# First batch's attention on four sets of buffers: q and k of all four jobs loaded ahead of v, the mask added by TensorE

## The chip, the cores and the metric

One Trainium2 chip, of which the kernel uses one core. The metric is the time of one execution on the device in microseconds (us). Three executions of the kernel before gave 918.25, 918.97 and 919.79 us; the median is 918.97 us.

## The reference

Inputs: q, k, v of shape (4 batches, 8 heads, 576 positions, 64), and the weights of two feed-forward layers, all float32.

```
q_d, k_d, v_d = means over 4 neighbouring positions          # 144 of them
out_d  = softmax(q_d k_d^T / 8) v_d ; out_up = each row of out_d repeated 4 times
mask   = |pos_i - pos_j| < 4
scores = where(mask, q k^T / 8, -1e9) ; out_local = softmax(scores) v
x = (out_up + out_local) laid out as (2304 tokens, 512)
x = (sigmoid(x Wg) * (x Wv)) Wo                              # layer 1, 1536 hidden
h = x Win ; out = (h * sigmoid(1.702 h)) Wout                # layer 2, 2048 hidden
```

So each batch first goes through a pooled (full) and a banded (local) attention, and the 2304 tokens then go through two gated layers. The large products are made as three float32r matmuls each (high times high, high times low, low times high).

## The kernel before, in words

**Two kinds of work.** The attention of batch b is four jobs, one for each pair of heads (`Job(b, hp)`, hp 0 to 3). A job loads q and k, pools them by four (`pool4`), makes the banded scores with 96 small matmuls (`scores`, L674), adds the mask and takes the softmax, makes the pooled scores with 8 matmuls (`down` or `pooled`, L724) and their softmax (`pooled_softmax`), transposes the pooled weights (`down_t`, L784), and multiplies both with v (`band`, L799, and `values`, L821). The sum of both (L834) is split into a high and a low part, `xhi` and `xlo` (L845, L847): slice hp of the input of layer 1. v of the first batch is pooled by 24 matmuls for each half of the heads (`Values.pool_tiles`, L592) with a matrix `ones`.

The layers are "visits". The first visit takes batch 0 through layer 1: for each of 12 pieces f of the hidden width, 24 matmuls of 512 columns make gate and value (`hidden`, L939 to L941, into `ph`), and 12 more the piece of the output (`result`, into `acc`). Each weight arrives as 64-bit words, is converted by ACT and DVE (`convert`, L865, L867, L869), and split into `whi` (ACT, L876) and `wlo` (DVE, L879). The attention of batches 1 to 3 is mixed into the visits before theirs.

**Where things lie.** Buffers are handed out in turn from named rings: `qt` and `kt` have two places each, `sc` one, `pt`, `tt`, `pd`, `xf`, `qd` and `kd` two, `pdt` and `half` one. Jobs 2 and 3 of batch 0 load q and k into the last four weight tiles (`qt0`, `kt0`), whose weights come later. All other buffers of batch 0 are those that later batches use.

**What sets the order.** `Plan` collects every operation with an engine, a cost, a due time and the buffers it reads and writes, and `Plan.order` lays them out one engine at a time by due times and its own costs; the program then holds that order on each engine. `T0` is the time for which the planner plans the first visit; `Job.t0`, `Job.due` and the constants at L514 ff. give the due times. Where the planner sees PE idle in the beginning it puts in fillers, bf16 matmuls on a tile `warm` whose result nobody reads (L1433). All loads and stores go through SP's queue, in the planner's order.

For a job of batch 0 the softmax of the band is: DVE adds the mask to the scores in PSUM and writes `sc` (L693), takes the maxima (L707), subtracts (L708); ACT takes the exponential into `pt` (L711); DVE sums (L712), inverts (L714), scales (L715) and transposes (L716) into `tt`.

```
            masked = self.b == 1
            def scored():
                for h in range(2 if masked else 0):
                    nc.tensor.matmul(ss.t[:, h, :n], identb.t, maskb, start=True, stop=False, skip_group_check=True)
```

In batch 1 (`masked`) the mask is instead put into PSUM by a matmul with the identity ahead of the scores (L668), and DVE reads maxima and differences from PSUM.

Of the kernel before, what the change touches and what calls it, by code (L numbers as in the profile page):

```python
# [288 lines left out]
def tile_multiscale_attention_gated_ffn(  # L289
# [9 lines left out]
    nc = tc.nc  # L299
# [86 lines left out]
    first = [x.rearrange("p a b -> p (a b)").bitcast(F32) for x in top[-4:]]  # L386
    firsts = [Slot(x[:, :n]) for x, n in zip(first, (S + 8, KPAD + S + 5) * 2)]
    plan.ring("qt0", firsts[::2])
    plan.ring("kt0", firsts[1::2])
    for n, x in enumerate(wslots[-8:]):  # L390
        x.under = (firsts[n // 2],)
# [8 lines left out]
    qslots, kslots, vslots, pslots = (plan.rings[nm][0] for nm in ("qt", "kt", "vt", "pt"))  # L400
# [70 lines left out]
    for s in [*qslots, *plan.rings["qt0"][0]]:  # L471
        nc.vector.memset(s.t[:, S:], 0.0)
    for s in [*kslots, *plan.rings["kt0"][0]]:
        nc.vector.memset(s.t[:, :KPAD], 0.0)
        nc.vector.memset(s.t[:, KPAD + S:], 0.0)
# [40 lines left out]
    T0 = 37.0e3  # L516
# [3 lines left out]
    EARLY = 16.0e3  # L520
    AHEAD = 15.0e3
    FIRST = ((-14.0e3, 14.0e3), (-13.0e3, 16.0e3), (-12.0e3, 18.0e3))
# [19 lines left out]
    class Values:  # L542
# [6 lines left out]
        def load(self):  # L549
            b, c = self.b, slice(self.c0, self.c0 + VC)  # L550
            if b:
                self.vt, self.vd, self.vg = buf("vt"), buf("vd"), buf("vg")

            hp = self.job.hp
            d, after = (self.job.t0 - 3000.0, self.job.t0 - 12000.0) if b else (4500.0 * hp, 4500.0 * hp)
            for kh in range(2) if b else ():
                dma(self.vg.t[:, kh], v[b, kh * 4 * GH:(kh + 1) * 4 * GH, c].rearrange("(g r) d -> g r d", r=4),
                    GH * 4 * VC * 4, [], [(self.vg, kh)], d, after)
            d, after = (self.job.due(0.2), self.job.t0 - 9000.0) if b else (4000.0 * hp, 4000.0 * hp)
            if not b:  # L560

                if hp:
                    return
                c, n, t, d, after = slice(0, DM), 2, vboth.rearrange("p g h c -> p g (h c)"), -19.2e3, 3.5e3
# [12 lines left out]
            row = NQ * (NT - 1) - 3  # L577
            dma(t[96:96 + S - row, NG - 1], v[b, row:S, c], (S - row) * n * VC * 4, [], [(x, 5) for x in bs],
                d, after)

        def pool_tiles(self):
# [3 lines left out]
            at = self.job.due(0.55)  # L585
# [22 lines left out]
    class Job:  # L608


        def __init__(self, b, hp):
            self.b, self.hp = b, hp
            if b == 0:
                a, z = -EARLY, T0 - EARLY
            else:
                a, z = visits[b - 1]["t"] - LEAD, visits[b]["t"] - (SLACK if b < B - 1 else SLACK7)
            step = (z - a) / NHP
            self.t0, self.t1 = a + hp * step, a + (hp + 1.6) * step
            self.banks = twos if b == 0 else twos[:1]
            self.merged = b > 0 and (b, hp) != (1, 0)  # L620
# [3 lines left out]

        def load(self):
            b, hp = self.b, self.hp
            early = b == 0 and hp > 1
            self.qt, self.kt = (buf("qt0"), buf("kt0")) if early else (buf("qt"), buf("kt"))
# [29 lines left out]
        def scores(self):  # L658
# [5 lines left out]
            masked = self.b == 1  # L664
# [15 lines left out]
            if not self.merged:  # L680
                op("pe", 1500.0 + 200.0 * masked, scored, [qt, kt, *[identb][:masked]], [ss, sc], when)
# [56 lines left out]
        def pooled_softmax(self, ss, c, at, masked):  # L738

            nmd, smd, pd = self.nmd, self.smd, self.pd  # L740
            op("dve", dve_ns(4 * G), lambda: nc.vector.reduce_max(
                nmd.t.rearrange("p (h r) -> p h r", h=2),
                ss.t[:GH, :, c:c + 2 * G].rearrange("p h (r k) -> p h r k", k=G), axis=AX.X),
               [ss, *masked], [nmd], at)
            op("act", 200.0, lambda: nc.scalar.mul(nmd.t, nmd.t, -SCALE_D), [], [nmd], at)
# [23 lines left out]
        def down_t(self):  # L769
            self.pdt = buf("pdt")  # L770
# [32 lines left out]
        def values(self):  # L803
# [21 lines left out]
            xf = buf("xf")  # L825
# [28 lines left out]

    def convert(src, out, due, at=None, after=None):

        w = buf("w64")
        if at is None:
# [3 lines left out]
        def words(n, dtype=I32):  # L862
# [3 lines left out]
            out.t.bitcast(F32), words(1, F32), AF.Prelu, scale=2.0 ** -112, alpha=-2.0 ** 32), [w], [out], due)  # L866
        op("act", act_ns(DM), lambda: nc.scalar.activation(  # L867
# [510 lines left out]
    def make_ones():  # L1378
        nc.gpsimd.memset(ones.t, 0.0)
        for i in range(4):  # L1380
            c = 30 + 36 * (i % 2)
            part = ones.t[32 * i:32 * i + 32, c:c + 6]
            nc.gpsimd.memset(part, 1.0)
            nc.gpsimd.affine_select(out=part, in_=part, pattern=[[-4, 6]], compare_op=ALU.is_ge,
                                    fill=0.0, base=-3, channel_multiplier=1)
            nc.gpsimd.affine_select(out=part, in_=part, pattern=[[4, 6]], compare_op=ALU.is_ge,
                                    fill=0.0, base=6, channel_multiplier=-1)

    op("pool", 1500.0, make_ones, [], [ones], -4.0e3)
# [89 lines left out]
```

## Time and profile before

| what | us |
|---|---|
| median of three executions (918.25 to 919.79) | 918.97 |
| the profiled execution, its own time | 919.47 |
| its span, first to last instruction | 917.8 |
| PE busy | 907.8 (99%) |
| DVE busy | 691.3 (75%) |
| ACT busy | 544.0 (59%) |
| POOL busy | 80.5 (9%) |
| chain that ended last: share of PE | 98% |

The busy time of an engine is the time in which an instruction of its own runs, whether anybody needs the result or not: PE's 907.8 us hold the fillers too. The profiled execution took 919.47 us, of which 917.8 us are its span and 1.67 us lie around it.

### The profile page before, as it was taken

The numbers are of one execution on the slowest core, as the hardware profiler recorded it, in microseconds if no ns is written. First come the engines' busy times: TensorE is split into PE (matmuls) and PEld (weight loads), VectorE is DVE, ScalarE is ACT, GpSimd is POOL, SyncE is SP. The second block draws the span as 40 slices with busy tenths as digits, with TensorE's granted clock in tenths as the row PEclk, the third lists the DMA queues.
The fourth block names the chain that finished last, engine by engine and source line by source line (L and its number), as shares of the span: only waits on it lengthen the run. The fifth ranks groups of instructions, "written<-read, shape, count | busy, mean of one in ns | idle before, by whom it ended". The sixth has DMA issues, their size and how long they took to land.

```text
span 917.8 us, 18930 instructions
## 1 busy us (share of the span) xinstructions
PE 907.8 (99%) x7392; PEld 761.9 (83%) x7392; DVE 691.3 (75%) x1291; ACT 544.0 (59%) x1163; POOL 80.5 (9%) x124
## 2 busy tenths in 40 slices
PE   8999999999999999999999999999999999999998
PEld 4678888888888887889999998888888988888886
DVE  4777776776576766799999898878976779877742
ACT  4788885656666666665545655545665655535541
POOL 6221100111011100010000000000301001000000
PEclk9999999999999999999999999999999999999999
DMA  9559672574365734434311751002531002000431
GB/s 286 139 193 261 197 216 57 164 213 148 126 190 181 237 116 145 153 109 141 108 51 41 223 196 46 37 33 73 193 125 70 1 1 69 35 35 35 167 98 47
DMA packets 63949, 113.76 MB, mean 124 GB/s; under 512 B 8241, under 2 KB 29563, under 8 KB 63858
## 3 DMA queue, kind: packets, MB, share of 16 engines
q1 hardware_dynamic: 63858, 112.54, 38.7%
q8 instruction: 58, 0.95, 0.4%
q14 instruction: 33, 0.27, 0.1%
HBM read 82.37 MB, written 30.15 MB: 123 GB/s over the span
## 4 chain that ended last, share of the span: by engine, by line
PE 98%; POOL 1%; issue 0%; DVE 0%; POOLq 0%
PE ph L939 14%; PE ph L940 13%; PE ph L941 13%; PE acc L939 9%; PE acc L941 8%; PE acc L940 8%; PE pa L940 7%; PE pa L939 7%; PE pa L941 7%; PE pa L799 2%; PE pa L674 1%; PE pa L724 1%; PE acc L1433 1%; PE pa L821 1%; PE pa L784 1%; PE acc L799 1%
## 5 line engine op out<-in xcount | busy, mean ns | idle before, releaser
L939 PE MATMUL ph<-xhi,whi 128*128 128x512 f32 (+1 forms) x344 | 135.1, 393 | 0.0
L940 PE MATMUL ph<-xhi,wlo 128*128 128x512 f32 (+1 forms) x344 | 131.6, 383 | 0.0
L941 PE MATMUL ph<-xlo,whi 128*128 128x512 f32 (+1 forms) x344 | 131.5, 382 | 0.0
L876 ACT CAST whi<-w 128x512 fp32r<-128x512 f32 x140 | 85.5, 612 | 59.9 <-PE ph L941 33.2
L879 DVE TENSOR_TENSOR wlo<-w,whi 128x512 fp32r<-128x512 f32 x137 | 95.4, 698 | 29.7 <-ACT whi L876 29.3
L879 DVE TENSOR_TENSOR wlo<-wr,whi 128x512 fp32r<-128x512 f32 x106 | 69.8, 660 | 41.2 <-ACT whi L876 39.9
L939 PEld LDWEIGHTS ph<-xhi,whi 128*128 128x128 f32 x344 | 64.7, 188 | 15.2 <-issue 2.1
L941 PEld LDWEIGHTS ph<-xlo,whi 128*128 128x128 f32 x344 | 64.8, 188 | 12.9
L876 ACT CAST whi<-wr 128x512 fp32r<-128x512 f32 x106 | 60.2, 570 | 25.2 <-PE acc L941 12.2
L940 PEld LDWEIGHTS ph<-xhi,wlo 128*128 128x128 f32 x344 | 64.9, 189 | 11.7
L939 PE MATMUL acc<-ghi,whi 128*128 128x512 f32 (+1 forms) x192 | 73.7, 384 | 0.0
L941 PE MATMUL acc<-glo,whi 128*128 128x512 f32 (+1 forms) x192 | 72.3, 377 | 0.5 <-DVE glo L879 0.5
L1053 DVE TENSOR_TENSOR w<-pa,w 128x512 f32<-128x512 f32 (+1 forms) x112 | 70.4, 629 | 2.4 <-PE pa L941 1.9
L940 PE MATMUL acc<-ghi,wlo 128*128 128x512 f32 (+1 forms) x192 | 72.2, 376 | 0.0
L876 ACT CAST w<-w 128x512 fp32r<-128x512 f32 x62 | 37.9, 619 | 43.1 <-PE acc L940 23.6
L940 PE MATMUL pa<-w,wlo 128*128 128x512 f32 (+1 forms) x166 | 60.6, 365 | 0.0
L941 PE MATMUL pa<-w,whi 128*128 128x512 f32 (+1 forms) x166 | 60.6, 365 | 0.0
L939 PE MATMUL pa<-w,whi 128*128 128x512 f32 (+1 forms) x166 | 60.6, 365 | 0.0
L879 DVE TENSOR_TENSOR w<-w,w 128x512 fp32r<-128x512 f32 x58 | 41.2, 716 | 19.0 <-ACT w L876 18.9
L973 ACT ACTIVATE th<-ph 128x512 f32<-128x512 f32 (+1 forms) x44 | 24.6, 559 | 39.2 <-PE ph L941 39.0
L978 DVE SCALAR_TENSOR_TENSOR th<-th,ph 128x512 f32<-128x512 f32 (+1 forms) x44 | 28.1, 638 | 24.5 <-PE ph L941 19.6
L867 ACT ACTIVATE w<-w 128x512 int32<-128x512 uint32 x68 | 45.2, 670 | 0.0
(281 smaller groups left out, 2222.5 us busy)
## 6 DMA issues: line engine op xcount, KB each, us to landing
w<-w SPq DMA_DIRECT2D x68, 512.0 KB
w2d<-we SPq DMA_DIRECT2D x32, 256.0 KB
w<-gd SPq DMA_DIRECT2D x32, 256.0 KB
gd<-w SPq DMA_DIRECT2D x30, 256.0 KB
st<-x2d SPq DMA_DIRECT2D x52, 128.0 KB
w<-w2d SPq DMA_DIRECT2D x16, 256.0 KB
wr<-w2d SPq DMA_DIRECT2D x16, 256.0 KB
qt<-qT SPq DMA_DIRECT2D x14, 288.0 KB
```

The costliest lines, as they stand in the source:

```text
L674: nc.tensor.matmul(ss.t[32 * i:32 * i + 32, h, g * NU:(g + 1) * NU], qt.t[hs, NQ * t:NQ * t + 32], kt.t[hs, NQ * t:NQ * t + NU], start=not ...
L724: nc.tensor.matmul(ss.t[:GH, h, c + r * G:c + (r + 1) * G], qd.t[h * D:(h + 1) * D, r * GH:(r + 1) * GH], kd.t[h * D:(h + 1) * D, :], star ...
L799: nc.tensor.matmul(ss.t[h * D:(h + 1) * D, s, q:q + NQ], vt.t[ks, g, v0 + h * D:v0 + (h + 1) * D], tt.t[ks, h, g, :NQ], start=True, stop=T ...
L867: op("act", act_ns(DM), lambda: nc.scalar.activation(words(0), words(0, U32), AF.Copy, scale=2.0 ** -29 * (1.0 - 2.0 ** -12), bias=2.0 ** ...
L876: op("act", act_ns(n), lambda: nc.scalar.copy(vh(), vm()), [rm], [rh], due)
L879: return lambda: on.tensor_sub(vl(), vm(), vh().bitcast(F32))
L939: nc.tensor.matmul(o, lhi, rhi, start=first, stop=False, skip_group_check=more)
L940: nc.tensor.matmul(o, llo, rhi, start=False, stop=False, skip_group_check=more)
L941: nc.tensor.matmul(o, lhi, rlo, start=False, stop=last, skip_group_check=more)
L973: op("act", act_ns(n, True), lambda h=h: nc.scalar.activation(th.t[:, :n], h.t[:, :n], AF.Tanh, scale=0.5 if layer == 1 else 1.702 / 4.0), ...
L978: op("dve", dve_ns(n), lambda: nc.vector.scalar_tensor_tensor(th.t[:, :n], th.t[:, :n], 1.0, hb[-1].t[:, :n], op0=ALU.add, op1=ALU.mult), ...
L1053: op("dve", dve_ns(N), lambda: nc.vector.tensor_add(tmp.t[:, o, :N], b.t[:, :N], tmp.t[:, i, :N]), [b, (tmp, i)], [(tmp, o)], t)
```

## The change

It touches the first batch alone, and the places and due times that go with it.

- **Buffers.** For batch 0 the rings `qt`, `kt`, `pt`, `tt`, `sc`, `nm`, `sm`, `pd`, `nmd`, `smd`, `xf` get two more places each (`sc` three, `pdt` one more), cut out of nine weight tiles (`wr5` to `wr7`, `w4` to `w9`); a new function `place` moves the weights of late pieces into those tiles.
- **Loads.** q and k of all four jobs come first on SP, then v.
- **Mask.** Batch 0 too puts the mask into PSUM by TensorE: two more matmuls for each job, and DVE's addition goes.
- **Engines.** `pool4` of jobs 0 and 3 becomes one sum by DVE in place of two additions by POOL. Job 3's pooled softmax subtracts, sums and scales on DVE, with one exponential on ACT for all four blocks. `ones` is made by DVE out of `ident`. Job 0 makes its pooled scores apart; jobs 1 to 3 of batch 0 make them right behind the banded scores ("merged"), as later batches do.
- **Weights of the first visit.** For every third weight one of ACT's two conversions (L867) becomes a shift on DVE (12 times).
- **Due times.** `T0` goes from 37 to 30 us; batch 0's jobs start 3 us apart, with 16 us each.

```diff
+    def place(f, part):
+        some = 2 * NRAW
+        if part == 2:
+            return some + f if f < 8 else 2 * NF1 + f
+        return 2 * f + part if f < some // 2 else 2 * f + part + 8
...
-            plan.ring(f"w{f}_{part}", [wslots[2 * NF1 + f if part == 2 else 2 * f + part]])
+            plan.ring(f"w{f}_{part}", [wslots[place(f, part)]])
...
+    over = [*low[-3:], *top[-6:]]
+    for n, x in enumerate(over):
+        if n < 3:
+            a, b_, c = parts_in(x, NS, 4 * G, 8 * NG)
+            some = [("sc", Slot(tiled(a))), ("pdt" if n == 2 else "pd", Slot(squares(b_)))]
...
+        elif n < 5:
+            some = [("xf", Slot(parts_in(x, S)[0]))]
+        else:
+            a, b_ = parts_in(x, NQK, NP)
+            some = [(("qt", "kt")[n % 2], Slot(a)), (("tt", "pt")[n % 2], Slot(tiled(b_)))]
...
+    for nm, some in early.items():
+        plan.ring(nm + "0", plan.rings[nm][0] + some)
...
-    T0 = 37.0e3
+    T0 = 30.0e3
+    STEP0 = 3.0e3
+    SPAN0 = 16.0e3
+    APOOL = (0, 1, 2)
+    QK0 = (0.0, 0.0, 2.4e3, 2.4e3)
+    V0 = 4.2e3
+    VPOOL = (0, 3)
+    LATER = 8.0e3
...
-    FIRST = ((-14.0e3, 14.0e3), (-13.0e3, 16.0e3), (-12.0e3, 18.0e3))
+    FIRST = ((-14.0e3, 9.0e3), (-13.0e3, 10.0e3), (-12.0e3, 11.0e3))
...
-            self.merged = b > 0 and (b, hp) != (1, 0)
+            self.merged = (b, hp) not in ((0, 0), (1, 0))
...
-                d, after = -20.0e3 + 500.0 * hp, (0.0, 0.0, 9.5e3, 12.0e3)[hp]
+                d, after = -20.0e3 + 500.0 * hp, QK0[hp]
...
         def pool4(self, dst, src, bsrc, due):
+            if self.b == 0 and self.hp in VPOOL:
+                op("dve", dve_ns(S), lambda: nc.vector.reduce_sum(
+                    dst.t, src.rearrange("p (g r) -> p g r", r=4), axis=AX.X), [bsrc], [dst], due)
+                return
...
-            masked = self.b == 1
+            masked = self.b <= 1
...
+            if self.b == 0 and self.hp not in APOOL:
...
+                op("dve", dve_ns(4 * G), lambda: nc.vector.tensor_sub(
+                    pd.t, ss.t[:GH, :, c:c + 2 * G].rearrange("p h (r k) -> p h r k", k=G),
+                    spread(nmd).rearrange("p (h r) q -> p h r q", h=2)), [ss, nmd], both, at)
+                op("act", act_ns(4 * G), lambda: nc.scalar.activation(flat, flat, AF.Exp, scale=SCALE_D),
+                   [], both, at)
+                op("dve", dve_ns(4 * G), lambda: nc.vector.reduce_sum(smd.t, flat, axis=AX.X), both, each, at)
+                op("dve", 305.0, inv, [], [smd], at)
+                op("dve", dve_ns(4 * G), lambda: nc.vector.tensor_mul(flat, flat, spread(smd)), [smd], both, at,
+                   port=True)
+                return
...
+        if nconv[0] % 3 == 2 and nconv[0] < 3 * NF1:
+            op("dve", dve_ns(DM, True), lambda: nc.vector.tensor_scalar(
+                out.t, out.t, 3, None, op0=ALU.logical_shift_left), [], [out], due, port=True)
+            op("dve", dve_ns(DM), lambda: nc.vector.scalar_tensor_tensor(
+                out.t, words(0), 29, out.t, op0=ALU.logical_shift_right, op1=ALU.bitwise_or), [w], [out], due, port=True)
+            return
...
+            nc.vector.reduce_sum(ones.t[x, c:c + 6], ident.t[x, 32 * i + 3:32 * i + 27].rearrange(
+                "p (j r) -> p j r", r=4), axis=AX.X)
```

Lines of the kernel with the change differ: its scores are L726, mask L720, pooled scores L777, pooled v L637, transposes L855, band L870, values L892, fillers L1509, large matmuls L1019 to L1021.

**The loads on SP.** Names: `qt0`, `qt1`, `w6` to `w9` are places for q and k, `vt` is v. Before, the start of SP's queue:

```order
L511 DMA qt0_121<-qT 128x576
L511 DMA kt0_123<-kT 128x576
L511 DMA qt1_122<-qT 128x576
L511 DMA kt1_124<-kT 128x576
L511 DMA vt_148<-v 32x5x512
L511 DMA vt_148<-v 32x6x512 x2
L511 DMA vt_148<-v 32x5x512
L511 DMA vt_148<-v 28x512
L511 DMA vt_148<-v 27x512
L511 DMA w6_117<-qT 128x576
L511 DMA w7_118<-kT 128x576
```

With the change:

```order
L549 DMA qt0_121<-qT 128x576
L549 DMA kt0_123<-kT 128x576
L549 DMA qt1_122<-qT 128x576
L549 DMA kt1_124<-kT 128x576
L549 DMA w7_118<-qT 128x576
L549 DMA w6_117<-kT 128x576
L549 DMA w9_120<-qT 128x576
L549 DMA w8_119<-kT 128x576
L549 DMA vt_148<-v 32x5x512
L549 DMA vt_148<-v 32x6x512 x2
```

The four loads of jobs 2 and 3 moved from behind v's six to ahead of them.

**DVE behind job 0's scores.** Job 0's scores lie in `pa0`, its pooled ones in `acc0`, job 1's scores in `acc1`; `small` and `smalld` hold maxima and sums. Before, from job 0's addition of the mask on:

```order
L693 TENSOR_TENSOR sc0_125<-pa0_159,mask_190 128x360
L707 TENSOR_REDUCE small_146<-sc0_125 128x12
L741 TENSOR_REDUCE smalld_147<-acc0_154 72x4
L708 TENSOR_TENSOR sc0_125<-sc0_125,small_146 128x360
L712 TENSOR_REDUCE small_146<-pt0_126 128x12
L714 RECIPROCAL small_146<-small_146 128x12
L715 TENSOR_TENSOR pt0_126<-pt0_126,small_146 128x12x30
L757 TENSOR_SCALAR smalld_147<-smalld_147 72x4
L758 RECIPROCAL smalld_147<-smalld_147 72x4
L716 STREAM_TRANSPOSE tt0_128<-pt0_126 128x384
```

With the change, the last 12 of the 21 rows from job 0's maxima (L760) to the pooling of job 3's k (L685 into `kd1`); `wr5`, `wr6` hold buffers of jobs 2 and 3 and job 1's differences, `w9` and `w8` q and k of job 3:

```order
L796 TENSOR_SCALAR smalld_147<-smalld_147 72x4
L797 RECIPROCAL smalld_147<-smalld_147 72x4
L761 TENSOR_TENSOR wr5_108<-acc1_155,small_146 128x360
L685 TENSOR_REDUCE qd1_133<-w9_120 128x144
L799 TENSOR_REDUCE wr5_108<-pa0_159 72x4
L760 TENSOR_REDUCE wr5_108<-pa0_159 128x12
L796 TENSOR_SCALAR smalld_147<-smalld_147 72x4
L797 RECIPROCAL smalld_147<-smalld_147 72x4
L765 TENSOR_REDUCE small_146<-pt1_127 128x12
L761 TENSOR_TENSOR wr6_109<-pa0_159,wr5_108 128x360
L767 RECIPROCAL small_146<-small_146 128x12
L685 TENSOR_REDUCE kd1_135<-w8_119 128x144
```

The addition of the mask is gone, work of three jobs alternates, and the pooling of job 3's q and k is DVE's.

**PE at the passage to the first visit.** Before, with the last rows of job 3's scores and the first of the visit:

```order
L674 MATMUL acc1_155<-w9_120,w8_119 32x30 x48
L1433 LDWEIGHTS warm_168
L1433 MATMUL ph1_150<-warm_168 128x512
L724 MATMUL pa0_159<-kd1_135,qd1_133 72x144 x4
L939 MATMUL ph0_149<-xhi0_89,whi0_78 128x512
L940 MATMUL ph0_149<-xhi0_89,wlo0_82 128x512
L941 MATMUL ph0_149<-xlo0_91,whi0_78 128x512
```

With the change:

```order
L1509 LDWEIGHTS warm_168
L1509 MATMUL ph1_150<-warm_168 128x512
L870 MATMUL acc1_155<-w9_120,vt_148 64x24 x24
L892 MATMUL acc1_155<-wr7_110,vd1_137 64x144 x4
L1019 MATMUL ph0_149<-xhi0_89,whi0_78 128x512
L1020 MATMUL ph0_149<-xhi0_89,wlo0_82 128x512
L1021 MATMUL ph0_149<-xlo0_91,whi0_78 128x512
```

The visit's first large matmul stood ahead of job 2's and job 3's transposes and bands, and now stands behind the last matmul of the whole first batch.

## Rows read from the trace of the kernel before

**Rows 1.** Windows: window, length; busy PE, PEld, DVE, ACT, POOL; clock, DMA, GB/s.

```profile
0.00:61.00 61.00, 55.65 (x1131) 36.29 (x1131) 41.71 (x93) 40.33 (x111) 25.83 (x58) 0.94 0.73 223
61.00:400.00 339.00, 339.00 (x3729) 274.22 (x3729) 237.85 (x416) 229.32 (x508) 29.97 (x44) 1.00 0.54 166
...
800.00:917.80 117.80, 113.63 (x502) 93.78 (x500) 69.85 (x114) 50.24 (x90) 1.53 (x1) 1.00 0.22 77
```

**Rows 2.** Windows of the filler tile warm alone: PE, PEld, DVE.

```profile
0.00:61.00 61.00, 19.32 (x64) 6.13 (x64) 0.11 (x1) 0.94 0.73 223
```

**Rows 3.** Timeline of PE at the start: start, length, instruction, idle before.

```profile
6.40 1.09 PE L674 MATMUL pa<-kt,qt 64*32 64x30 f32 x96
...
7.74 0.71 PE L724 MATMUL acc<-kd,qd 64*72 64x144 f32 x8
...
13.35 1.07 PE L724 MATMUL pa<-kd,qd 64*72 64x144 f32 x8 [3.27 <-POOL kd L640]
```

**Rows 4.** Timeline of PE, 16 to 26 us: the small matmuls behind the scores.

```profile
16.66 2.95 PE L592 MATMUL acc<-vt,ones 64*72 64x256 f32 x24
19.54 0.39 PE L1433 MATMUL acc<-warm 128*128 128x512 bf16 x1
19.77 0.67 PE L784 MATMUL acc<-ident,pd 72*72 72x72 f32 x8
20.27 0.38 PE L1433 MATMUL ph<-warm 128*128 128x512 bf16 x1
20.58 2.81 PE L592 MATMUL pa<-vt,ones 64*72 64x256 f32 x24
...
23.65 0.89 PE L799 MATMUL acc<-tt,vt 30*64 30x24 f32 x48
24.47 0.71 PE L821 MATMUL acc<-pdt,vd 72*64 72x144 f32 x8
25.11 0.39 PE L1433 MATMUL acc<-warm 128*128 128x512 bf16 x1
```

**Rows 5.** Timeline of PE: mask and scores of batch 1's first job.

```profile
43.32 0.32 PE L668 MATMUL pa<-mask,identb 128*128 128x180 bf16 x2
43.57 1.02 PE L674 MATMUL pa<-kt,qt 64*32 64x30 f32 x96
```

**Rows 6.** Timeline of PE: first output piece, second hidden piece, second output piece.

```profile
60.98 0.58 PE L939 MATMUL acc<-ghi,whi 128*128 128x512 f32 x1
...
63.94 0.39 PE L939 MATMUL ph<-xhi,whi 128*128 128x512 f32 x1
...
69.38 0.39 PE L939 MATMUL acc<-ghi,whi 128*128 128x512 f32 x1
```

**Rows 7.** Timeline of DVE: last memset, then pieces of job 0's softmax.

```profile
3.81 0.07 DVE L481 MEMSET pt<- 128x12 f32 x1
...
8.62 0.74 DVE L741 TENSOR_REDUCE smalld<-acc 72x4 f32<-72x576 f32 x1
...
10.89 0.54 DVE L712 TENSOR_REDUCE small<-pt 128x12 f32<-128x372 f32 x1 [1.09 <-ACT pt L711]
11.47 0.23 DVE L714 RECIPROCAL small<-small 128x12 f32<-128x12 f32 x1
```

**Rows 8.** Timeline of DVE: maxima and differences of batch 1's first job, from PSUM.

```profile
45.22 0.53 DVE L707 TENSOR_REDUCE small<-pa 128x12 f32<-128x360 f32 x1
...
47.73 0.53 DVE L708 TENSOR_TENSOR sc<-pa,small 128x360 f32<-128x360 f32 x1
```

**Rows 9.** Windows, columns as in rows 1: the low clock, and the DMA rates.

```profile
15.00:16.00 1.00, 1.00 (x96) 1.00 (x96) 0.22 (x1) 0.72 (x4) 0.41 (x1) 0.50 1.06 399
6.00:14.00 8.00, 4.73 (x122) 2.76 (x120) 4.65 (x10) 3.03 (x13) 6.16 (x19) 0.97 1.07 229
```

**Rows 10.** Timeline of POOL: pooling job 0's k by two additions.

```profile
5.85 0.67 POOL L638 TENSOR_TENSOR half<-kt 128x288 f32<-128x288 f32 x1
6.59 0.43 POOL L640 TENSOR_TENSOR kd<-half 128x144 f32<-128x144 f32 x1
```

More of the change, by code (lines that the diff above doesn't have):

```diff
@@ L384, in tile_multiscale_attention_gated_ffn, with parts_in, tiled, squares @@
         aslots += ring(nm, n, shape, F32, apool)
[L386 to L391, printed above, removed]
+    def parts_in(x, *sizes):
+        flat, at, out_ = x.rearrange("p a b -> p (a b)").bitcast(F32), 0, []
+        for n in sizes:
+            out_.append(flat[:, at:at + n])
+            at += n
+        return out_
+    def tiled(x):
+        return x.rearrange("p (h g c) -> p h g c", h=2, g=NG)
+    def squares(x):
+        return x[:GH].rearrange("p (h r q) -> p h r q", h=2, r=2)
+    NS, NP, NQK = 2 * NG * NU, 2 * NG * 32, S + 8
+    early = collections.defaultdict(list)
+    over = [*low[-3:], *top[-6:]]
[3 more added lines that the diff above has]
+            some = [("sc", Slot(tiled(a))), ("pdt" if n == 2 else "pd", Slot(squares(b_)))]
+            if n < 2:
+                for i, nm in enumerate(("nm", "sm", "nmd", "smd")):
+                    y = c[:, i * 2 * NG:(i + 1) * 2 * NG].rearrange("p (h g) -> p h g", h=2) if i < 2 else \
+                        c[:GH, 4 * NG + 4 * (i - 2):4 * NG + 4 * (i - 1)]
+                    some.append((nm, Slot(y)))
+        elif n < 5:
[3 more added lines that the diff above has]
+            some = [(("qt", "kt")[n % 2], Slot(a)), (("tt", "pt")[n % 2], Slot(tiled(b_)))]
+        for nm, slot in some:
+            early[nm].append(slot)
+        for w_ in wslots:
+            if w_.tile.tensor is x.tensor:
+                w_.under = tuple(slot for _, slot in some)
     small = apool.tile([P, 4, 2, NG], F32, name="small", tag="small")
@@ L399, in tile_multiscale_attention_gated_ffn @@
     aslots += plan.rings["vt"][0]
-    qslots, kslots, vslots, pslots = (plan.rings[nm][0] for nm in ("qt", "kt", "vt", "pt"))
+    qslots, kslots, vslots, pslots = (plan.rings[nm][0] for nm in ("qt0", "kt0", "vt", "pt0"))
     NREG = 14
@@ L470, in tile_multiscale_attention_gated_ffn @@
     nc.vector.memset(warm, 0.0)
-    for s in [*qslots, *plan.rings["qt0"][0]]:
+    for s in qslots:
         nc.vector.memset(s.t[:, S:], 0.0)
-    for s in [*kslots, *plan.rings["kt0"][0]]:
+    for s in kslots:
         nc.vector.memset(s.t[:, :KPAD], 0.0)
@@ L563, in load @@
                     return
-                c, n, t, d, after = slice(0, DM), 2, vboth.rearrange("p g h c -> p g (h c)"), -19.2e3, 3.5e3
+                c, n, t, d, after = slice(0, DM), 2, vboth.rearrange("p g h c -> p g (h c)"), -19.2e3, V0
                 bs = [self.vt, halves[0, 1].vt]
@@ L584, in pool_tiles @@
             vt, vd = self.vt, self.vd
-            at = self.job.due(0.55)
+            at = self.job.due(0.55) if self.job.hp == 0 else self.job.due(0.2)
             ss = bank(self.job.banks)
@@ L680, in scores @@
             if not self.merged:
-                op("pe", 1500.0 + 200.0 * masked, scored, [qt, kt, *[identb][:masked]], [ss, sc], when)
+                op("pe", 1500.0 + 200.0 * masked, scored, [qt, kt, *[identb][:masked]], [ss, sc], when,
+                   T0 + LATER if self.b else 0.0)
             else:
@@ L740, in pooled_softmax, with inv @@
             nmd, smd, pd = self.nmd, self.smd, self.pd
+            def inv():
+                nc.vector.tensor_scalar_add(smd.t, smd.t, 1.0e-9)
+                nc.vector.reciprocal(smd.t, smd.t)
             op("dve", dve_ns(4 * G), lambda: nc.vector.reduce_max(
@@ L744, in pooled_softmax, with spread @@
                [ss, *masked], [nmd], at)
+            if self.b == 0 and self.hp not in APOOL:
+                flat = pd.t.rearrange("p h r q -> p (h r) q")
+                both, each = [(pd, 0), (pd, 1)], [(smd, 0), (smd, 1)]
+                def spread(x):
+                    return x.t[:, :, None].to_broadcast([GH, 4, G])
+                op("dve", dve_ns(4 * G), lambda: nc.vector.tensor_sub(
[8 more added lines that the diff above has]
+                return
             op("act", 200.0, lambda: nc.scalar.mul(nmd.t, nmd.t, -SCALE_D), [], [nmd], at)
@@ L769, in down_t @@
         def down_t(self):
[L770 removed]
+            self.pdt = self.buf("pdt")
             ss = self.ss = bank(self.banks)
@@ L853, in tile_multiscale_attention_gated_ffn @@
     wt = {}
+    nconv = [0]
     def convert(src, out, due, at=None, after=None):
         w = buf("w64")
+        nconv[0] += 1
         if at is None:
@@ L1378, in make_ones @@
     def make_ones():
-        nc.gpsimd.memset(ones.t, 0.0)
+        nc.vector.memset(ones.t, 0.0)
         for i in range(4):
[L1381 to L1389, printed above, removed]
+            c, x = 30 + 36 * (i % 2), slice(32 * i, 32 * i + 32)
+            nc.vector.reduce_sum(ones.t[x, c:c + 6], ident.t[x, 32 * i + 3:32 * i + 27].rearrange(
+                "p (j r) -> p j r", r=4), axis=AX.X)
+    op("dve", 700.0, make_ones, [ident], [ones], -20.0e3)
     op("act", act_ns(P), lambda: nc.scalar.copy(identb.t, ident.t), [ident], [identb], 0.0)
```

17 lines of the change are left out of this document (8 added, 9 removed).

## The prediction

> **What bounds the kernel now.** I read the windows by stage first. From 61 to 400 us PE is busy for 339.00 of 339.00 us at the full clock, DVE for 237.85 and ACT for 229.32 (70% and 68%), and the last stretch differs little [rows 1]. There the time is PE's work, and that work stays: both orders hold the same large matmuls, and from the 132nd on the small ones of later batches stand between the same large ones. So the change can win or lose only before PE is saturated, unless a later wait appears where none is now. My mark for saturation is the first matmul of the first output piece: 60.98 us [rows 6]; 48 large matmuls stand ahead of it in either order. Of the first 61 us PE is busy for 55.65 [rows 1], 19.32 of them with fillers [rows 2]. The rest is idle: 5.35 us. No change of the start can bring more than these 24.7 us.
>
> The timeline of PE then shows where they go. One idle stretch of 3.27 us ends when POOL has pooled job 1's k [rows 3]; the other places are fillers between jobs that wait for each other's buffers.
>
> **The change, step by step.** I follow the chain through the new order with durations of these rows.
>
> *First scores.* The loads of jobs 0 and 1 keep their places, and so do PE's first 13 fillers. The mask's two matmuls put 0.25 us (start to start, [rows 5]) ahead of scores that started at 6.40 and took 1.09 [rows 3]: they end at 7.74, and DVE starts on them at 7.85 with a tenth for the handoff. DVE is free by then: its memsets end at 3.88 [rows 7]; four more take about 1 us (two pairs like this one), `ones` half a us, two poolings 1.5.
>
> *The pooling on DVE* (L685) is not in this trace. Its ends are 0.54 us, a sum of 372 elements [rows 7], and 1.10, the two additions of POOL that it replaces [rows 10]. I take 0.74, the row that reads as many elements (576, [rows 7]).
>
> *DVE up to job 3's pooled k*, 21 instructions: three maxima and three differences of 360 elements at 0.53 [rows 8], 3.18; three pooled maxima at 0.74, 2.22; two sums at 0.54, 1.08; six reciprocals and other small ones at 0.23, 1.38; one scaling and one transpose like those, 0.53 and 0.54; two poolings, 1.48 [rows 7]. Sum 10.4: DVE is there at 18.3. ACT's exponentials for jobs 0 and 1 lie beside this; a wait for them would come on top.
>
> The mask through PSUM makes DVE read maxima and differences from PSUM in place of SBUF. The rows from PSUM take 0.53 us each [rows 8], and I count no difference. [...]
>
> *PE then* makes job 3's pooled scores (0.71 at the full clock, [rows 3]) and a filler (0.31, [rows 4]): it starts on v's pooling at 19.3. PE alone would be there at 17.7: 6.40, four times 0.25, 1.02 and 0.71 [rows 3, 5], and 13 wide and 6 narrow fillers (0.23 and about 0.06, [rows 4]). v must have landed: 1.52 MB behind 2.36 MB of q and k. While v came DMA moved 229 GB/s, with q and k alone 399 [rows 9]; started at 2 us, v lands between 14.6 (each at its rate) and 18.9 us (all at 229). It is covered, narrowly at the far end.
>
> *PE's small matmuls* up to the first visit, start to start [rows 4]: two poolings of v at 2.88, 5.8; four groups of transposes at 0.50, 2.0; eight of the band at 0.82, 6.6; four of values at 0.64, 2.6; ten fillers at 0.23 to 0.31, 2.7. Sum 19.6 (rounded terms: 19.7), so 38.9 us. PE should not wait here: DVE's next 20 instructions, at the same prices 9.7 us, end with job 3's transposed weights at 28, and PE comes to them at about 34. Behind PE's last small matmul slice 3 needs a copy, the addition, and its two parts, some 2.6 us on ACT and DVE: 41.5. PE first has nine large matmuls of slices 0 and 1, 2.0 us at 0.227 (24 of them from 63.94 to 69.38, [rows 6]), and a filler, mask and scores of batch 1, 1.6 [rows 4, 5]: 42.5. That cover is 1 us; what slice 3 is later than that, PE waits.
>
> *To the mark:* 39 more large matmuls, 8.9 us: 51.4. Before, PE had at the mark also done pooled scores of batch 1 (0.71), which now come later: like with like, 60.98 - 0.71 = 60.3 against 51.4. **The gain is 8.9 us.**
>
> *Edits costed at nothing.* The 12 shifts that go from ACT to DVE: at most 0.74 us each like DVE's longest row here [rows 7], 9 us, in a stretch where DVE has 101 us free [rows 1]. The new places: their weights are converted only after batch 0 is done. POOL loses work. On SP batch 1's v waits for batch 0's bands (PE at 34 to 39), and one weight load stands behind it, eight more follow; it goes out at about 37 and ACT comes to it at about 45. Were that cover gone, the third hidden piece would be late by the rest.
>
> **The sum:** 919.47 - 8.9 = **910.6 us**, against the profiled execution's own time, which is 0.5 above the median of the runs.
>
> **The rivals.**
>
> *Weights late (chance 0.12).* PE now asks for weights ten us sooner, with ACT and DVE straight out of batch 0. For it: the cover of 1 us above. Against it: at 70% and 68% [rows 1] they catch up while PE works. A wait of 2 to 3 us: 913.
>
> *v late (0.08).* Should 3.88 MB move at 200 GB/s, a little under the lower row [rows 9], v lands at 21.4, 2.1 us behind PE: 912.7.
>
> *DVE becomes the bound (0.08), the slower side.* By the order, DVE has before the mark about as much work as now, 42 us (41.71 in 61 us, 68%, [rows 1]); the forecast needs it busy for 82% of 51.4 us. If it stays as held up as now, by ACT between its own instructions and by POOL on the same operands, the mark is at 42/0.68 = 61.8, 1.5 us behind 60.3: 921; at 66% it is 63.6: 922.8. It decides from 42/60.3 = 70% downward. Against it: today's gaps are waits for one job's next step, like the 1.09 us for ACT's exponential [rows 7], and now three jobs alternate.
>
> *The clock (0.05).* [...]
>
> **How the numbers follow.** A change under 0.2% (1.8 us) can't be told from none. Forecast 0.67, between 909.0 (PE alone sets v's pooling, at 17.7) and 912. Range: the low end with the 0.5 us to the median, 908.4; the high end takes in late weights, late v and the upper price of the poolings (0.7 us), 914.5. Left out are DVE as bound, the clock and what is worse than I price. Faster: forecast, both late cases and a little of the clock, 0.89; same: most of the clock and DVE near 70%, 0.05; slower: DVE, 0.06.
>
> **What would show it.** v's pooling on PE at 18 to 20 us without an idle stretch over 2 us before; the first large matmul near 39; the mark near 51.4; no idle PE to 400 us. Wrong in its step: DVE's poolings above 1.1 us, v's pooling released by DMA, a large matmul released by `xlo` or `wlo` with PE idle for over 1 us, a clock of 0.50 behind 20 us. The forecast as a whole is wrong if the mark is at 51 and the time is not near 910, or the mark is behind 58.

## The result, and the profile after

The changed kernel takes 928.04 us (median of 6 executions, 922.92 to 929.38) against 919.12 (median of 6, 918.25 to 920.32) for the kernel before: ratio 1.0089, 95% interval 1.0065 to 1.0114, wholly above 1. It is slower by 9 us; 910.6 was forecast. The profiled execution took 927.03 us (its span is 925.3), 7.56 more than the profiled execution of before.

First the page: engines, then PE's granted clock in 40 slices of the span (23 us each).

```profile
PE 913.1 (99%) x7380; PEld 766.6 (83%) x7380; DVE 695.1 (75%) x1318; ACT 535.2 (58%) x1139; POOL 67.2 (7%) x100
...
PEclk8879999999999999999999999999999999999999
```

Only the first three slices are below the rest. The windows by stage, which answer to [rows 1], say the same:

```profile
0.00:67.45 67.45, 59.94 (x1110) 40.98 (x1111) 42.76 (x104) 34.27 (x86) 17.03 (x37) 0.80 0.61 186
...
60.00:400.00 340.00, 340.00 (x3738) 274.47 (x3737) 240.50 (x427) 227.67 (x508) 25.28 (x40) 1.00 0.57 170
```

Behind the start PE is as saturated as before. The mark, the first matmul of the first output piece, stands at 67.45 us; it stood at 60.98 [rows 6], or 60.27 like with like. The 7.2 us between are nearly the whole difference of the two executions. So the method (only the start can change) held, and the start went wrong. PE's waits, of the whole execution, longest first:

```profile
PE acc L777 <- issue: 5.1, 1, 5.1
PE acc L637 <- issue: 1.5, 1, 1.5
PE acc L1509 <- DVE warm L508: 1.0, 1, 1.0
PE acc L1021 <- DVE glo L959: 0.5, 1, 0.5
```

The two longest are put down to "issue": PE waited for nothing that the profile shows. The timeline of PE has them in the middle of groups whose operands were there; the wait for POOL's pooled k [rows 3] is gone:

```profile
9.97 0.46 PE L777 MATMUL acc<-kd,qd 64*72 64x144 f32 x3
15.50 0.88 PE L777 MATMUL acc<-kd,qd 64*72 64x144 f32 x5 [5.07 <-issue]
...
24.44 2.38 PE L637 MATMUL acc<-vt,ones 64*72 64x256 f32 x20
28.28 0.66 PE L637 MATMUL acc<-vt,ones 64*72 64x256 f32 x4 [1.45 <-issue]
```

The first stop comes behind the third of eight matmuls of job 1's pooled scores. DVE then waits 5.56 us for that group and ACT 5.93 us for DVE: the three engines stand. The clock falls with this stop: it is 0.50 from 13.5 to 20.3 us. (The row of a window has its bounds and length; busy PE, PEld, DVE, ACT, POOL; granted clock, DMA share, GB/s.)

```profile
14.00:20.00 6.00, 4.50 (x116) 3.07 (x115) 2.86 (x7) 1.42 (x8) 0.00 (x0) 0.50 1.05 340
```

The second loss shows in the windows behind the second stop (28.28 us):

```profile
28.28:37.00 8.72, 8.72 (x193) 5.91 (x193) 6.34 (x14) 6.97 (x14) 0.00 (x0) 1.00 0.27 93
37.00:38.00 1.00, 1.00 (x32) 0.93 (x24) 0.00 (x1) 0.58 (x2) 0.00 (x0) 0.67 0.54 213
38.00:52.00 14.00, 14.00 (x279) 10.64 (x277) 5.01 (x8) 5.69 (x11) 3.06 (x2) 0.50 0.48 144
```

PE is busy for 8.72 of 8.72 us with small matmuls and one filler between groups, and the granted clock falls from 1.00 to 0.50 all the same. It stays there for the rest of the small matmuls and is back only behind the first large ones. The groups by form, from 28 to 37 us and from 39 to 52 us, give the price of one matmul at either level (the mean in ns, last number before the second bar):

```profile
L870 PE MATMUL pa<-tt,vt 30*64 30x24 f32 x48 | 0.9, 213 | 0.0
L892 PE MATMUL pa<-pdt,vd 72*64 72x144 f32 x8 | 0.7, 299 | 0.0
```

```profile
L870 PE MATMUL pa<-tt,vt 30*64 30x24 f32 x48 | 1.5, 278 | 0.0
L892 PE MATMUL acc<-pdt,vd 72*64 72x144 f32 x8 | 1.2, 461 | 0.0
```

And the timeline has the large ones before and after the return:

```profile
54.33 0.63 PE L1020 MATMUL ph<-xhi,wlo 128*128 128x512 f32 x1
...
58.74 0.40 PE L1020 MATMUL ph<-xhi,wlo 128*128 128x512 f32 x1
```

### The profile page after: what moved, and what is told of

Read it like the earlier page. It is cut to its first block, busy times and chain, and to the rows that moved or that the text cites. A ratio compares the mean times of both kernels' runs of the same rounds, so it can differ in the third digit from the quotient of the medians.

```text
span 925.3 us, 18880 instructions
## 1 busy us (share of the span) xinstructions
PE 913.1 (99%) x7380; PEld 766.6 (83%) x7380; DVE 695.1 (75%) x1318; ACT 535.2 (58%) x1139; POOL 67.2 (7%) x100
## 4 chain that ended last, share of the span: by engine, by line
PE 98%; issue 1%; DVE 0%
PE ph L1019 14%; PE ph L1021 13%; PE ph L1020 13%; PE acc L1019 9%; PE acc L1021 8%; PE acc L1020 8%; PE pa L1019 7%; PE pa L1021 7%; PE pa L1020 7%; PE pa L870 2%; PE pa L726 1%; PE acc L1509 1%; PE pa L777 1%; PE pa L892 1%; PE pa L855 1%; PE acc L870 1%
## 5 line engine op out<-in xcount | busy, mean ns | idle before, releaser
L1019 PE MATMUL ph<-xhi,whi 128*128 128x512 f32 (+1 forms) x344 | 135.1, 393 | 0.0
L1021 PE MATMUL ph<-xlo,whi 128*128 128x512 f32 (+1 forms) x344 | 132.1, 384 | 0.0
L959 DVE TENSOR_TENSOR wlo<-w,whi 128x512 fp32r<-128x512 f32 x137 | 95.0, 695 | 29.1 <-ACT whi L956 28.6
L959 DVE TENSOR_TENSOR wlo<-wr,whi 128x512 fp32r<-128x512 f32 x106 | 67.3, 638 | 37.4 <-ACT whi L956 36.3
L1019 PEld LDWEIGHTS ph<-xhi,whi 128*128 128x128 f32 x344 | 65.0, 189 | 15.2 <-issue 2.1
L1021 PEld LDWEIGHTS ph<-xlo,whi 128*128 128x128 f32 x344 | 65.1, 189 | 13.1
L1019 PE MATMUL acc<-ghi,whi 128*128 128x512 f32 (+1 forms) x192 | 73.7, 384 | 0.0
L1021 PE MATMUL acc<-glo,whi 128*128 128x512 f32 (+1 forms) x192 | 72.3, 377 | 0.5 <-DVE glo L959 0.5
L1019 PE MATMUL pa<-w,whi 128*128 128x512 f32 (+1 forms) x166 | 60.7, 366 | 0.1
L1021 PE MATMUL pa<-w,whi 128*128 128x512 f32 (+1 forms) x166 | 60.6, 365 | 0.0
L1019 PEld LDWEIGHTS acc<-ghi,whi 128*128 128x128 f32 x192 | 36.0, 188 | 7.3 <-issue 1.7
```

The costliest lines, as they stand in the source:

```text
L959: return lambda: on.tensor_sub(vl(), vm(), vh().bitcast(F32))
L1019: nc.tensor.matmul(o, lhi, rhi, start=first, stop=False, skip_group_check=more)
L1021: nc.tensor.matmul(o, lhi, rlo, start=False, stop=last, skip_group_check=more)
```

## The experiments

Theory 1 has two separate causes. (a) PE stops because the next block of its own instructions has not come: the block is fetched by a transfer that queues behind the data. (b) The long stretch of small matmuls lets the clock fall at 37 us. Theory 2: this fall is an after-effect of the stops, so there is one cause.

The page gives (a) its first support. PE's instructions have a queue of their own:

```profile
q1 hardware_dynamic: 63858, 112.54, 39.2%
q8 instruction: 58, 0.95, 0.4%
```

0.95 MB in 58 packets are 16 KB each; PE ran 7380 matmuls and as many weight loads, 254 to a packet. Adding up the counts in the timeline, the two stops stand behind 222 and 476 matmuls: 254 matmuls with their loads, 508 instructions; with 4 semaphore instructions of the trace between them 512, two packets apart. The kernel before has one such stop, 1.01 us, behind 604 matmuls, one packet further:

```profile
31.32 0.76 PE L799 MATMUL pa<-tt,vt 30*64 30x24 f32 x36
33.10 0.41 PE L799 MATMUL pa<-tt,vt 30*64 30x24 f32 x12 [1.01 <-issue]
```

**The place of the stop.** The first twelve wide fillers (512 columns) are cut into 48 narrow ones (128 columns):

```diff
-                            done += [filler] * n
+                            if filler is fillers[0] and t < 6.0e3:
+                                done += [fillers[1]] * (4 * n)
+                            else:
+                                done += [filler] * n
```

> The changed kernel with the first twelve wide fillers cut into 48 of 128 columns, so that PE has 36 more matmuls (each with its weight load) behind it at any later point. Theory 1 (PE stops because the next block of its instructions has not come): the stop is tied to the number of instructions behind it, so it comes 36 matmuls earlier in the order, inside job 1's scores with about 60 of 96 done, near 9.7 us, and ends near 15 us; the second stop also comes 36 matmuls earlier, inside job 3's pooled scores or the fillers and first matmuls of v's pooling. Rival (something in job 1's pooled scores, their bank or operands holds PE): the stop stays in those pooled scores after 3 of 8 matmuls, at 10.4.

Measured: one execution, 931.20 us. The timeline of PE:

```profile
8.97 0.74 PE L729 MATMUL acc<-kt,qt 64*32 64x30 f32 x63
14.63 0.47 PE L729 MATMUL acc<-kt,qt 64*32 64x30 f32 x33 [4.92 <-issue]
...
21.75 0.36 PE L729 MATMUL pa<-w,w 64*32 64x30 f32 x16 [2.89 <-issue]
```

The stop moved to 63 of 96 scores: again 222 matmuls from the start, exactly 36 earlier in the order. The next one stands 128 matmuls later, and a third (0.63 us) 127 after that. Where PE stops is set by how many instructions lie behind it; the rival falls.

**What the block waits for.** v's loads, and the weight loads behind them on SP, wait for a write of DVE into v's tile that stands behind job 0's differences:

```diff
+    HOLD = 10.3e3
...
-    FIRST = ((-14.0e3, 9.0e3), (-13.0e3, 10.0e3), (-12.0e3, 11.0e3))
+    FIRST = ((-14.0e3, 13.0e3), (-13.0e3, 14.0e3), (-12.0e3, 15.0e3))
...
+    vhold = [halves[0, n].vt for n in range(2)]
+    op("dve", 80.0, lambda: nc.vector.memset(vboth[:, 1:2, :, :2], 0.0), [], vhold, -20.0e3, HOLD)
     halves[0, 0].load()
```

> The changed kernel with v's loads, and the weight loads behind them, held back until DVE has made job 0's differences (near 9 us), so that the block of instructions asked for near 7.4 us has only q and k ahead of it. Theory 1: the instruction packet lands near 10 us in place of 12.7, PE goes on near 12.5 to 13 and the first stop is 2 to 3 us in place of 5.07; v lands near 17, still ahead of PE; v's pooling on PE starts 2 to 3 us earlier (near 22); the clock still falls behind v's pooling, so mark 64 to 66 and time 924 to 926. Theory 2 (the fall follows from the long stop): the fall is shorter or gone. Rival for the stop (not tied to the traffic of transfers): it stays at 5 us.

Measured: 923.68 us, ratio 1.0030 (1.0015 to 1.0045). The DMA view of one microsecond, for the changed kernel from 12 to 13 us and for this one from 8 to 9 (in each the only microsecond from 6 to 13 us in which an instruction packet begins; a row has packets, MB, and the time that the packets took as a share of 16 engines' microsecond):

```profile
q1 hardware_dynamic: 136, 0.26, 106.1%
q8 instruction: 1, 0.02, 8.4%
```

```profile
q1 hardware_dynamic: 122, 0.24, 61.5%
q8 instruction: 1, 0.02, 6.6%
```

And PE in this kernel:

```profile
10.87 0.52 PE L778 MATMUL acc<-kd,qd 64*72 64x144 f32 x5 [0.81 <-issue]
...
18.17 0.99 PE L727 MATMUL acc<-w,w 64*32 64x30 f32 x94 [2.70 <-issue]
```

With v held back the packet begins at 8.4 in place of 12.7 (narrower windows give this), and it takes 1.06 us in place of 1.34 (the shares above, of 16 us). When the block is asked for no row shows; the expectation's 7.4 us are an estimate. PE starts its 94th matmul at 7.3 us in the changed kernel, 128 ahead of the 222nd; and behind 700 us, at DMA shares of 0.08 to 0.39, that kernel's last nine packets begin 128 to 136 matmuls ahead of their places (222, and 127.3 more for each packet, from the stops at 222 and 604). The first stop shrinks from 5.07 to 0.81 at the same matmul, further than the 2 to 3 us expected. PE goes on 2.5 us behind the packet's start, 1.4 behind its end; in the changed kernel it was 2.8 and 1.5. A new stop of 2.70 us comes 127 matmuls later, while v is moving. In all thirteen kernels, 31 stops, PE goes on 2.3 to 3.0 us behind a packet's start and 1.2 to 1.6 us behind its end.

The clock still falls, in all ten executions (mean 0.986 to 0.989). In the profiled one it is 0.50 from 19.5 to 22.9 us, behind the second stop, and again from 33.1 us on. This second fall comes 15 us behind the last stop, in the changed kernel 9 us, and in both just as job 1's values begin (33.0 and 37.2 us): it goes with the place in the order rather than with the time since a stop. That speaks against theory 2. The mark is 64.2, in the range expected; the time is a little below its range.

**The clock.** Extra wide fillers ahead of each small group behind v's pooling; the planner's times don't see them, so nothing else moves. One more per group, then two:

```diff
-                            done += [filler] * n
+                            done += [filler] * (n + (self.MORE.get(o, 0) if filler is fillers[0] else 0))
...
+        if self.b == 0:
+            plan.MORE[o_] = 1
```

> The changed kernel with nine more wide fillers, one ahead of each small group of batch 0 behind v's pooling; nothing else moves. Theory 1 (the clock falls at 37 us because too little of this stretch is wide work; the two stops of PE are a separate matter): the granted clock stays at 1.00 from 22 to 60 us; nine fillers at 0.23 us cost 2.1 us, the lower level gives back 9.0: mark 67.45 + 2.1 - 9.0 = 60.5, time near 920. Both stops of PE stay where they are (10.4 to 15.5, 26.8 to 28.3). Theory 2 (the fall at 37 us follows from the stops): the clock falls as before, mark 70 or later, time near 930.

> As the run with nine, but eighteen more wide fillers, two ahead of each group. Theory 1: if nine hold the clock, eighteen cost 2.1 us more than nine and nothing is gained: mark 62.6, time near 922; if nine do not hold it, eighteen may, and this run is the faster of the two by up to 7 us. Theory 2: the clock falls all the same, mark 72 or later, time 932.

Measured: 923.65 us with nine (ratio 1.0043, 1.0015 to 1.0072), 924.63 with eighteen (1.0045, 1.0029 to 1.0061). In the profiled execution with nine the stops are 4.34, 0.45 and 3.10 us, longer together than in the changed kernel, and yet the clock holds behind 32.1 us (windows):

```profile
24.00:32.00 8.00, 4.90 (x31) 2.46 (x29) 5.07 (x14) 4.03 (x10) 2.19 (x4) 0.80 0.24 49
36.00:44.00 8.00, 8.00 (x260) 5.77 (x252) 3.25 (x5) 6.37 (x13) 1.08 (x1) 1.00 0.59 192
44.00:52.00 8.00, 8.00 (x195) 5.78 (x187) 4.57 (x7) 4.68 (x11) 2.95 (x3) 1.00 0.72 200
```

Its mark is 62.6, not 60.5: the stops took 7.9 us in place of 6.5, and the clock was not at 1.00 all the way from 22 us. It was at 0.50 from 28.7 to 32.1 us, behind the stop of 3.10 (the 0.80 of the first row). With eighteen the mark is 65.7 and not 62.6, behind stops of 6.09 and 2.19. A short fall like this one, 3.4 to 6.8 us, follows most of the longer stops in these traces, also the first stop of the changed kernel; so far theory 2 is right. For the long fall at 37 us it fails here: longer stops, no such fall. What I had not expected is that the fall is not the same in every execution. Taking a mean granted clock of 0.99 or more as "held", the changed kernel held in 0 of 6, with nine more fillers in 7 of 10 (median of those about 922.7, the others 929.0 to 930.7), with eighteen in 10 of 10. On the chip of these two runs the kernel with v held back and no filler more held it in 0 of 10.

The other direction, no filler at all in this stretch:

```diff
+            plan.MORE[o_] = -1
```

> The changed kernel without the nine wide fillers that it has behind v's pooling (one ahead of each small group). Theory 1 (wide work holds the clock): the clock falls sooner than 37 us, near 31 to 34, and comes back only behind the first large matmuls; nine fillers less save 2 to 4.5 us, the longer stretch at the lower level costs 2 to 3: mark 65 to 67.5. Rival (the fillers do nothing for the clock, the level is set otherwise): the fall stays at 37 to 38 us and the mark is 63 to 64.

Measured: 926.79 us in one execution, mark 67.2, stops 4.07, 0.92 and 3.10. The clock fell twice (windows):

```profile
30.00:32.00 2.00, 2.00 (x9) 0.92 (x9) 0.65 (x2) 1.67 (x4) 0.00 (x0) 0.50 0.03 8
36.00:38.00 2.00, 2.00 (x72) 1.77 (x74) 0.00 (x0) 1.73 (x4) 0.00 (x0) 1.00 0.81 281
40.00:42.00 2.00, 2.00 (x56) 1.88 (x52) 0.45 (x1) 1.21 (x3) 0.00 (x0) 0.50 0.34 51
```

It was 0.50 from 28.6 to 35.4 us, behind the third stop (6.8 us; 3.4 with nine more fillers, behind a stop of the same length), and again from 38.8 to 55.9. The long fall came hardly later than with one filler per group; that part of my expectation is wrong. The mark is inside its range by other terms: the stops grew by 1.6 us, and the second pooling of v, at the lower level, took 5.10 in place of 2.81. Against the long fall one filler per group was as good as none here; two hold in most executions.

**Both edits together**, in five versions: the hold of the fourth run or a release one step sooner (HOLD = 6.2e3, behind DVE's pooling of job 0's k), with fillers ahead of all groups or only of those with band and values.

> The two edits that each helped, together: v's loads and the weight loads held behind DVE's differences of job 0, and nine more wide fillers behind v's pooling. If the two losses are separate (theory 1), the gains add: stops of about 0.8 and 2.7 us as with the hold alone, the granted clock at 1.00 from 24 to 60 us, mark 64.2 + 2.1 - 9.0 = 57.3, time 923.7 - 6.9 = 917, which is 3 us under the kernel before. If they share a cause, the mark stays at 61 to 63 and the time at 920 to 922.

> As the run with both edits, but v's loads are released one step sooner, behind DVE's pooling of job 0's k (near 7.2 us), just when PE asks for its next block. Theory 1: the first block is still ahead of v, so the first stop stays at 1 to 1.5 us; v ends 1.5 us sooner and the second block with it, so the second stop is 1.0 to 1.7 in place of 2.7: mark near 56.3, time near 916. If v's packets get in ahead of the first block, the first stop is 3 to 5 us and the time 918 to 920.

> As the run with the earlier release, but with five more fillers in place of nine: ahead of the groups that hold band and values, not of those with the transposes. If five are enough to hold the clock, the mark is 0.9 us earlier than with nine (near 55.4); if not, the clock falls between 35 and 50 us and the mark is 3 to 8 us later.

> The hold of v as first tried (behind DVE's differences of job 0, near 9 us), with five more fillers behind v's pooling, ahead of the groups with band and values. Stops of 0.8 and 2.7 to 3.0 us whatever the clock does. Theory 1 with a clock that is not the same in every execution: executions with a mean granted clock of 0.996 or more end near 916.8 (0.9 under those of the run with nine), those with a fall near 924; fewer fillers than nine, so at most half of them hold, and the median is 918 to 924. If the number of fillers does not matter and something else decided in the run with five fillers and the earlier release, nearly all hold and the median is 917.

> The same hold, with ten more fillers, two more ahead of each group with band and values. Theory 1 (more wide work holds the clock in more executions): as many or more executions hold as with nine spread over all groups (6 of 12 there); those that hold end near 918, and the median is 918 to 920, under the kernel before. If the fall does not depend on the number of fillers: half of them fall again, the median is 921.

Measured ("held" as above; the mark is that of the profiled execution; the first three versions ran on one chip, the last two on another):

| edit | median us (range) | ratio to before (95%) | held | mark |
|---|---|---|---|---|
| hold, 9 more fillers | 920.99 (916.61 to 930.13) | 1.0010 (0.9982 to 1.0037) | 6 of 12 | 66.1 |
| sooner release, 9 more | 919.99 (916.61 to 927.75) | 1.0004 (0.9986 to 1.0022) | 11 of 12 | 60.3 |
| sooner release, 5 more | 918.16 (916.17 to 923.05) | 0.9983 (0.9969 to 0.9998) | 10 of 10 | 61.1 |
| hold, 5 more | 917.37 (915.40 to 924.41) | 0.9980 (0.9956 to 1.0005) | 9 of 12 | 56.3 |
| hold, 10 more | 918.14 (916.81 to 925.19) | 0.9993 (0.9973 to 1.0012) | 10 of 12 | 57.9 |

One of the ten in the third row lies at the bound (923.05 us, mean clock 0.990).

The gains add: with the hold and nine fillers the six executions that held took 916.6 to 918.5, where 917 was expected, the six others 923.5 to 930.1. The profiled one is of the latter (windows):

```profile
36.00:38.00 2.00, 1.87 (x54) 1.73 (x48) 1.01 (x2) 1.21 (x3) 0.72 (x1) 0.76 0.23 61
38.00:44.00 6.00, 6.00 (x111) 4.11 (x109) 1.96 (x3) 1.82 (x3) 2.14 (x2) 0.50 0.70 206
```

The sooner release was a miss: the first packet began at 9.2 us (8.7 with the hold and nine fillers) and the second at 18.1 (16.1), and the stops were 1.90, 2.51 and 1.54 us where 1 to 1.5 and 1.0 to 1.7 were expected; in the run with five fillers they were 1.73, 2.23 and 3.37. That v's packets got ahead of the block fits this, but was not tried by itself. How often the clock holds does not go by the number of fillers alone: on one chip nine held in 6 of 12 with the hold and in 11 of 12 with the sooner release, and five in 10 of 10. On the other chip five held in 9 of 12, where at most half were expected, and ten in 10 of 12. What decides it in one execution stays open.

The sooner release with five fillers is the one version whose interval lies below the kernel before (by 1.7 us of medians), and it is some 10 us below the changed kernel. One of five versions, with an upper end of 0.9998, is thin evidence for a gain. The best execution of all, 915.40 us, is of the hold with five. Its timeline and window:

```profile
10.94 0.52 PE L779 MATMUL acc<-kd,qd 64*72 64x144 f32 x5 [1.12 <-issue]
...
17.97 0.99 PE L728 MATMUL acc<-w,w 64*32 64x30 f32 x94 [2.42 <-issue]
...
24.10 0.37 PE L639 MATMUL acc<-vt,ones 64*72 64x256 f32 x1 [1.37 <-issue]
...
42.56 0.50 PE L1025 MATMUL ph<-xhi,whi 128*128 128x512 f32 x1
```

```profile
28.00:42.50 14.50, 14.50 (x459) 10.64 (x457) 8.26 (x15) 11.24 (x22) 4.33 (x4) 1.00 0.66 179
```

**One part undone.** POOL pools q and k of jobs 0 and 3 again:

```diff
-    VPOOL = (0, 3)
+    VPOOL = ()
```

> The changed kernel with one part undone: job 0's q and k and job 3's are pooled on POOL again, not on DVE. Theory 1 (early on the block of instructions sets the time, so a sooner pooled k only turns a wait for POOL into a wait for the block): PE waits 1 to 3 us for POOL's pooled k, the stop for the block is shorter by about as much, and PE comes to v's pooling at 24 to 25.5 us (24.44 now); the clock falls as before; mark 67 to 69, time 927 to 929. If the DVE pooling was worth its time: v's pooling at 26.5 or later, mark over 70, time over 930.

Measured: 924.89 us in one execution, mark 65.3. PE comes to v's pooling at 24.46, as expected, against 24.44 in the changed kernel:

```profile
10.31 0.34 PE L777 MATMUL pa<-kd,qd 64*72 64x144 f32 x1
15.40 1.24 PE L777 MATMUL pa<-kd,qd 64*72 64x144 f32 x7 [4.75 <-issue]
...
24.46 2.81 PE L637 MATMUL acc<-vt,ones 64*72 64x256 f32 x24
```

The wait for POOL that I expected is not there: both pooled k were ready when PE came to them (7.97 and 10.31 us), PE ran into the same stop (222 matmuls again) and lost nearly the same time. The mark is earlier than expected because the next stop is short (0.62 us), none falls into v's pooling, and the long fall ends at 54.8 in place of 57.8 us. The time lies inside the range of the changed kernel's six executions. So in this execution a sooner pooled k bought nothing while the block was late.

## Why the prediction was wrong

PE's order and the costs of the steps were as forecast; the forecast had no term for PE's instructions and gave the clock a chance of 0.05. Step by step:

- *First scores end 7.74.* Measured 7.65 (6.63 and 1.02). Right.
- *The pooling on DVE, 0.74.* Measured 0.74 and 0.75. Right, as are maxima from PSUM at 0.53; in the kernel before, job 0's maxima over 360 elements took 0.53 us from SBUF too (at 8.18 us).
- *DVE at job 3's pooled k at 18.3.* Measured 23.4; without the 5.56 us for which DVE waited for the stopped group, 17.9. Right but for the stop.
- *"It starts on v's pooling at 19.3."* Measured 24.44. **This step failed**: 5.14 us, of which the first stop is 5.07. That the rest is so small is partly luck. From 15.50 to 24.44 PE had no idle stretch: its own way, 17.7 alone, took 1.7 us more beside the stop, much of it at the clock of 0.50 behind it (scores 1.21 us at 17.89, 1.02 at 22.52), and the 1.6 us that the sum had kept for a wait for DVE covered this. The kernel before had the same block to wait for, but PE reached it later. PE there spent 3.27 us waiting for POOL's k [rows 3] and got to its 222nd matmul near 16 us, with its packet begun at 13.0 and in at 14.4. I counted that wait as time to be won. It was also the time in which the block came, and once it was gone the block, begun at 12.7, was late. The sign stood in the trace that I had: of its 5.35 us of idle PE, 1.01 are the stop at 33.10, without a releaser, which I passed over.
- *"Sum 19.6", the small matmuls at the full clock.* **This failed too.** They took 28.0 us (24.44 to 52.45): 1.45 for the second stop, and 7.0 that I put down to the lower clock. Group by group it is 6.5: the rows from 37.24 on took 15.2 us, at the full-clock times of the same groups 8.7; the rest is rounding of my terms. Behind them the nine large matmuls, a filler, mask and scores took 5.95 in place of 3.6: another 2.35 at the lower clock. From there to the mark 9.05, forecast 8.9.
- The sum: 5.14 + 1.45 + 6.96 + 2.35 + 0.15 = 16.05, which is 67.45 - 51.4.
- *The clock rival* is the one that came, and its chance was wrong. Its time of 916.5 to 920.5 was an estimate: all small matmuls at 1.3 to 1.5 times their time, 6 to 10 us, from two groups of the kernel before that ran, all but 0.2 us, at a granted clock of 0.50 (13.6 to 17.0 us): scores at 1.30 us (at 14.89) against 1.02 [rows 5] and pooled scores at 1.07 against 0.71 [rows 3]. Measured are 9.3 us, or 8.9 with the 6.5. That this is so near is partly luck: the clock fell only at 37.3 us, the groups behind it took 1.75 times their time (15.2 to 8.7), and 2.35 us fell on large matmuls and batch 1's first scores. What I held against this rival was that the new order has no idle stretch above 1.6 us (17.7 to 19.3). That ties the clock to PE's idle time. The trace shows the fall at 37 us behind 8.72 us without any, and fillers, not shorter stops, prevented it. I should have asked what the kernel before had in this stretch that the new one lacks: between its small groups stand large matmuls and up to six fillers, and the new order takes these away together with the idle time. And the kernel before itself lost its clock behind an idle stretch of only 1.01 us, the stop at 33.10:

```profile
34.10:37.40 3.30, 3.30 (x78) 2.33 (x75) 2.60 (x7) 1.86 (x6) 2.28 (x3) 0.50 1.06 232
```

- *Weights late, v late:* neither showed. No large matmul waits on a weight; no v pooling waits on DMA. (By the rows of its six loads v is 1.55 MB, not 1.52; this moves its landing by 0.1 to 0.2 us.) *DVE as bound:* DVE was busy for 42.76 us before the mark, the 42 that I had, 63% of it; but it was waiting for PE and not PE for it.
- Two of the signs of being wrong named the right places: a clock of 0.50 behind 20 us, and a mark behind 58.

With both losses small the order comes near its sum: in the best execution the mark is at 56.3. Less the three stops (4.9) and the five fillers (1.1) that is 50.3, where 51.4 was forecast. This is a subtraction and no run, and part of the difference is a clock that rose sooner in this execution (its first 13 fillers took 4.16 us in place of 5.41). No version here got rid of the stops, so the gain of 8.9 us was seen in none.

## What to carry to other kernels

A wait that you take out may have been covering a transfer that no line of the program shows; count PE's instructions to the places where it will run fastest (48 f32 matmuls of the program are 96 matmuls and 96 weight loads here), and look at what its instruction packets queue behind. Fillers between small matmuls are not only waste, and stray large matmuls may not be either (no run here tried them alone): before a reordering removes them, ask for the granted clock of the stretch that is left, and do not read a busy PE as a safe clock. Where a time falls into two groups, read the clock of each execution before comparing medians.

## What the hardware showed that I had not expected

- PE runs out of instructions: stops of 0.4 to 6.1 us, all at 222, 350, 476 or 604 matmuls from the start (within one), whatever group stands there. In the changed kernel 254 matmuls and weight loads come to a packet, and PE stopped at two of 58 packets; the first of these stops, beside full data queues (DMA share 1.05 to 1.06 from 8 to 14 us), cost 5.07 us.
- PE goes on 1.2 to 1.6 us after the packet's end (2.3 to 3.0 after its start), in stops of 0.8 us as in those of 5; so even an early packet has this much behind it.
- The granted clock fell to 0.50 with PE busy without a gap, and at the lower level small matmuls took 1.3 to 1.5 times as long each (213 to 278 ns, 299 to 461) and large ones 0.63 in place of 0.40 us; from start to start, which is what the path sees, a group of the band took 1.42 us in place of 0.83. The short falls (3.4 to 6.8 us) came behind stops; the row from 28.28 to 37.00 has no wait, and the long fall came at its end all the same.
- The same kernel kept the clock in some executions and lost it in others, 6 to 6 in one version, with some 7 us between the two halves.
